# One accumulator tile a bank through the expert stage, with its padding columns written by a product

## The chip, the cores and the metric

The kernel runs on 1 core of a Trainium2 chip. The metric is the device time of one execution in microseconds (us). Engines are named as in the profile: PE is TensorE's matmul, PEld its weight load, DVE VectorE, ACT ScalarE, POOL GpSimd, SP the engine that issues most DMAs.

## What is computed

A decayed linear attention feeds a mixture of experts. The attention's 3072 rows of 512 are routed each to the one expert of eight with the largest logit:

```python
for t in range(S):
    state = gamma[None, :, None, None] * state + np.einsum('bhd,bhe->bhde', k[:, :, t], v[:, :, t])
    y[:, :, t] = scale * np.einsum('bhd,bhde->bhe', q[:, :, t], state)
...
expert_idx = np.argmax(logits, axis=1)
...
for e in range(E):
    mask = expert_idx == e
    h = np.maximum(x[mask] @ w1[e], 0.0)          # w1[e]: 512 x 1024
    out[mask] = gate_w[mask, None] * (h @ w2[e])  # w2[e]: 1024 x 512
```

## The kernel before

The attention runs over 12 blocks of 256 tokens while logits, ranks and a table of slots are made. Then the experts follow one after the other, sorted by their row counts (expert 0 stays first), with room for CAPS = 408, 408, 400, 392, 384, 384, 360, 360 rows. Each engine works through its instructions in the order of the code (`manual_schedule`); only semaphores between engines set the times.

Every float32 product is made of three: weights and activations are split into a high part (`whi`, `xh`, `hh`; cast on ACT) and a low part (`wlo`, `xl`, `hl`; subtraction on DVE), and high x high, high x low and low x high are summed. The weights come in 64 pieces of 512 KB (per expert four of w1, then four of w2), which `load_piece` issues on SP into four buffers `raw`, and which `split` casts on ACT (L217) and subtracts on DVE (L223). A new load into a buffer waits for the L223 that read it.

An expert's first layer makes 8 groups (`ft`) of 12 products (L238) into one accumulator bank each; `hidden` reads it with a relu on ACT (L244, gives `hh`) and then on DVE (L245, gives `hl`). The second layer has two forms. `layer2` makes 4 groups (`dt`) of 24 products (L1021) with the tokens along the columns; `y_turn` (L1027) then transposes the accumulator on DVE in blocks of 32 columns, and so reads up to the next multiple of 32 (288 for 280, 416 for 408). `layer2_rows` (L1063) makes rows directly and needs no transposition. `layer2` is used for experts 0, 1, 2, 3 and 6 (`TURNED`), and for the first 280 rows (`EARLY`) of expert 0.

Accumulators come from `acc_()`: it takes six of the eight PSUM banks in turn (py0, py1, pst0, pst1, b0, b1), and each call makes a new tile in its bank, whose first writer waits until all that used the old tile of the bank are done. The columns between the row count and the next multiple of 32 are cleared by a DVE memset before the products: L1079 for the four `layer2` groups of expert 0 (`early_acc`, 8 columns), L1212 for experts 1, 2, 3 and 6 (four memsets each, of 8, 16, 24 and 24 columns, at `ft` = 6, ahead of `hidden(6)`). As DVE works in order and the memset is the first writer of the tile, the first product of the group waits for all that stands ahead of the memset on DVE.

The order of expert 0's end (L1082 to L1149), in which the work below stands: `layer2` dt 0, then `y_turn` and the remaining `sort_steps` (small DVE operations), dt 1, dt 2; transposes of the late 128 rows (`xr0`, L608 on PE); `split` of piece 8; two groups of the late rows' first layer (L1103, `hr`) with `split` of piece 9 and the gates between them; `turn_hidden(0)` (L1116 on PE, L1118 on ACT, L1119 on DVE); `split` of piece 10; `layer2` dt 3; `turn_hidden(1)`; `split` of piece 11; `x_turn` and `x_low` of expert 1 (L1004, L1005, L1011: they transpose and split the gathered rows `xg`); `layer2_rows` of the late rows; `y_turn(3)`; 16 DMAs of `out_rows` (L1033). Expert 1's rows reach `xg` by gathers (L589, POOL), a write to DRAM (L975) and a reading back (L994), both on SP.

In the loop over experts 1 to 7 (L1177) the next expert's rows are turned and three of its weight pieces split inside the second layer (`next_x`), ahead of `y_turn` on DVE.

Of the kernel before, what the change touches and what calls it, by code (L numbers as in the profile page):

```python
# [13 lines left out]
BF16 = mybir.dt.bfloat16  # L14
# [10 lines left out]
P = 128  # L25
# [11 lines left out]
Q = 32  # L37
# [4 lines left out]
NXC = -(-CAP // Q)  # L42
OV = 352
EARLY = 280
# [61 lines left out]
def retention_moe(ctx: ExitStack, tc: tile.TileContext, q, k, v, emb, tau, w1, w2, const, const16, out):  # L106
    nc = tc.nc

    cp = ctx.enter_context(tc.tile_pool(name="cp", bufs=1))
# [42 lines left out]
    def bank(tag, bufs=1):  # L152
        return ps_.tile([P, 512], F32, name=tag, bufs=bufs)


    turn_of = ["b0", "b1", "b2", "b3"]
    npt, nacc = [-1], [-1]

    def pt_():
        npt[0] += 1  # L160
# [1 line left out]

    def acc_():
        nacc[0] += 1
        return bank(("py0", "py1", "pst0", "pst1", "b0", "b1")[nacc[0] % 6])


    NPC = NE * 8
# [11 lines left out]
    def load_piece(behind=None):  # L180
        g = nload[0]
        if g >= NPC:
            return
        nload[0] += 1
        s, j = divmod(g, 8)
        e = expert[s]
        r = rp.tile([P, 1024], F32, name="raw")
        if s == 0 and j < 4:

            for jj in range(KT):  # L190
                f = P * jj + Q * j
                nc.sync.dma_start(out=r[jj * Q:(jj + 1) * Q], in_=w1[0, f:f + Q, :])
        elif j < 4:
            i = nc.sync.dma_start(out=r, in_=w1r[ds(e * DM + j * P, P), :])
            if behind is not None:
                after(i, behind)
        else:
            i = nc.sync.dma_start(
                out=r.rearrange("p (c d) -> p c d", c=2),
                in_=w2r[ds(e * DF + 2 * (j - 4) * P, 2 * P), :].rearrange("(c p) d -> p c d", p=P))  # L200
            if behind is not None:
                after(i, behind)
        raw_t[g] = r
# [22 lines left out]
    def split():  # L226
        split_cast()()

    def first_layer(e, ft, acc, xh, xl, cols, whole=KT):
        w = cols.stop - cols.start  # L230
        for kt in range(KT):
            wh, wl = piece[e * 8 + kt]
            f = slice(ft * P, (ft + 1) * P)
            terms = ((wh, xh), (wh, xl), (wl, xh))
            if kt >= whole:
                terms = ((wholes[e * 8 + kt], xh.bitcast(F32)), (wh, xl))
            for i, (a, x) in enumerate(terms):
                nc.tensor.matmul(acc[:, :w], a[:, f], x[:, kt, cols], start=(kt + i == 0),  # L238
                                 stop=(kt == KT - 1 and i == len(terms) - 1))
                yield  # L240
# [326 lines left out]
    def run_all(*gs):  # L567
        gs = list(gs)
        while gs:
            gs = [g for g in gs if next(g, gs) is not gs]  # L570
# [14 lines left out]
    def tokens(p, e, c):  # L585
        nc.gpsimd.tensor_copy(out=si[:p, e, c], in_=tb[:p, e, c, 1])
# [299 lines left out]
    hh0 = hp.tile([P, FT, CAP], F32R, name="hh")  # L886
    hl0 = hp.tile([P, FT, CAP], F32R, name="hl")
# [14 lines left out]
    def slots(e):  # L902
        if e not in expert:
            load_expert(e)
        nc.sync.dma_start(out=tb[:, e], in_=tbl[ds(expert[e] * STRIDE, NG * P), :2 + NE].rearrange("(j p) o -> p j o", p=P))
# [65 lines left out]
    def write_rows(e):  # L971
        full, rest = full_rest(e)
        xr, xs = xrs[e], xsd[e % 2]
        for j in range(full if e == 1 else 0):
            nc.sync.dma_start(out=xs[j * P:(j + 1) * P], in_=xr[:, j])  # L975
        if e > 1:
            nc.sync.dma_start(out=xs[:full * P].rearrange("(j p) x -> p j x", p=P), in_=xr[:, :full])
        if rest:
            nc.sync.dma_start(out=xs[full * P:full * P + rest], in_=xr[:rest, full])
# [7 lines left out]
    def gates_of(e):  # L987
        return gates(e, [(P, slice(0, NG), tb[:, e, :, 2:])])
# [25 lines left out]
    def layer2(e, dt, hh, hl, c, acc=None):  # L1014
        acc = acc_() if acc is None else acc
        n = 0
        for kt in range(FT):
            wh, wl = piece[e * 8 + 4 + kt // 2]
            f = slice((2 * dt + kt % 2) * P, (2 * dt + kt % 2 + 1) * P)
            for a, x in ((wh, hh), (wh, hl), (wl, hh)):  # L1020
                nc.tensor.matmul(acc[:, :c], a[:, f], x[:, kt, :c], start=(n == 0), stop=(n == 3 * FT - 1))  # L1021
                n += 1
        return acc

    def y_turn(dt, acc, yt, c):
        nb = -(-c // Q)
        nc.vector.transpose(out=yt[:, :nb, dt], in_=acc[:, :nb * Q].rearrange("p (n b) -> p n b", b=Q))  # L1027
# [46 lines left out]
    gather_rows(1)  # L1074
    tokens(P, 0, slice(3, 4))
    tokens(P, 1, slice(0, NG))
    def early_acc():
        acc = acc_()
        nc.vector.memset(acc[:, EARLY:-(-EARLY // Q) * Q], 0.0)  # L1079
        return acc  # L1080

    for dt in range(3):  # L1082
        acc = layer2(0, dt, hh0, hl0, EARLY, early_acc())
        y_turn(dt, acc, yt0, EARLY)
        if dt == 0:
            run_all(sort_steps)
# [10 lines left out]
    for f in (slice(0, 512), slice(512, 1024)):  # L1097
        acc = acc_()
# [13 lines left out]
    def turn_hidden(f):  # L1112
        ps = pt_()
        o = ps.rearrange("p (k t) -> p k t", k=4)
        for i in range(4):
            nc.tensor.transpose(o[:, i], hr[:, (4 * f + i) * P:(4 * f + i + 1) * P], ident)  # L1116
        kk = slice(4 * f, 4 * f + 4)
        nc.scalar.copy(out=hh0[:, kk, late], in_=o)  # L1118
        nc.vector.tensor_tensor(out=hl0[:, kk, late], in0=o, in1=hh0[:, kk, late].bitcast(F32), op=ALU.subtract)  # L1119

    turn_hidden(0)
    split()
    load_piece()
    acc = layer2(0, 3, hh0, hl0, EARLY, early_acc())
    turn_hidden(1)
    split()
    load_piece()
# [10 lines left out]
    acc = acc2  # L1138
# [38 lines left out]
    for e in range(1, NE):  # L1177
        nxt = e + 1 < NE
        c = CAPS[e]
        cols = slice(0, c)  # L1180
        hh = hp.tile([P, FT, CAP], F32R, name="hh")
        hl = hp.tile([P, FT, CAP], F32R, name="hl")
        gsteps = iter(())
        last = None
        for ft in range(FT):
            acc = last or acc_()
            for _ in first_layer(e, ft, acc, *xTs[e], cols):
                pass
            if ft == 0 and e + 2 < NE:
                slots(e + 2)  # L1190
            if nxt and ft == 1:
                write_rows(e + 1)
            if not nxt and ft == 2:
                nc.gpsimd.drain()
            if ft in (0, 1, 3, 5, 6):
                split()
                load_piece()
            if pend and not pend[5] and ft < 4:
                out_rows(pend[1], pend[2], ft, pend[3])
            if nxt and ft == 3:  # L1200
                read_quarters(e + 1)
            if ft == 1:
                gsteps = gates_of(e)
                next(gsteps)
            if ft > 2:
                for _ in range(3):
                    next(gsteps, None)
            if ft == FT - 2 and TURNED[e]:
                last, *accs = [acc_() for _ in range(KT + 1)]
                if c % Q:  # L1210
                    for a in accs:
                        nc.vector.memset(a[:, c:-(-c // Q) * Q], 0.0)  # L1212
            hidden(ft, acc, hh, hl, cols)
        done, pend = pend, None

        def finish_two():
            if done:
                for j, n in done[4][:2]:
                    finish(done[0], j, n, done[2])
                del done[4][:2]  # L1220

        og = mp.tile([P, NG, DM], F32, name="og", bufs=2)
        if TURNED[e]:
            yt = mp.tile([P, NXC, KT, Q], F32, name="yt", bufs=2)
            for dt in range(KT):
                acc = layer2(e, dt, hh, hl, c, accs[dt])
                if dt < 2:
                    finish_two()
                if dt < 2:
                    squares(e + 1, dt)  # L1230
                if dt < 3:
                    next_x(e + 1, dt)
                if dt == 1:
                    next_rows(e + 2)
                y_turn(dt, acc, yt, c)
            pend = (e, yt, og, c, groups_of(e), False)
        else:
            for j, n in groups_of(e):
                acc = layer2_rows(e, j, n, hh, hl, slice(j * P, j * P + n))
                finish_two()  # L1240
                if nxt:
                    if j < 2:
                        squares(e + 1, j)
                    next_x(e + 1, j)
                    if j == 1:
                        next_rows(e + 2)
                finish(e, j, n, og, acc[:n])
# [90 lines left out]
```

## Time and profile before

| | us |
|---|---|
| median of 3 runs | 421.93 (420.23 to 426.4) |
| the profiled execution | 419.81 |
| its span in the trace | 418.0 |
| around the span (419.81 - 418.0) | 1.8 |
| PE busy | 393.6 (94%) |
| DVE busy | 255.2 (61%) |
| ACT busy | 211.5 (51%) |

An engine's busy time is the time in which it had an instruction under way. PE's is no measure of its speed: the granted clock of a stretch stands beside it (1.00 is 2.4 GHz, 0.50 is 1.2 GHz). A wait is put down to the releaser that came last.

### The profile page before, as it was taken

Reading aid. Unit: us, or ns where it says so; the run is one execution under the profiler, and the core shown is the slowest. Engines: PE = TensorE matmul, PEld = TensorE weight load, DVE = VectorE, ACT = ScalarE, POOL = GpSimd, SP = SyncE. Lnnn points to the kernel's source line nnn. Section 1 sums busy time; section 2 is a strip of 40 time slices with the busy share of each in tenths; the row PEclk is TensorE's granted clock in tenths of the full one; section 3 lists DMA queues with packets and bytes.
Section 4 is the critical chain, followed back from the end, with each engine's and each line's share of the span. In section 5 each row is a group of like instructions: output and inputs, shape, how many; then the busy total and the mean of one; then the engine's idle time right before and its main releaser. Section 6 shows DMA issues by size and latency. Waiting matters only on the chain.

```text
span 418.0 us, 9549 instructions
## 1 busy us (share of the span) xinstructions
PE 393.6 (94%) x3648; PEld 360.0 (86%) x3648; DVE 255.2 (61%) x546; ACT 211.5 (51%) x378; POOL 157.3 (38%) x176
## 2 busy tenths in 40 slices
PE   7999999999987796997999999999999999999993
PEld 3998889888876676897999999999889989999971
DVE  4497877879788243762676296186376474775400
ACT  3565567557746033644544565375475465643410
POOL 2567485788562310151260260161147053000130
PEclk9999999999999898999999999999999999999997
DMA  7898998986677963269596977969778958941121
GB/s 224 252 295 258 255 266 247 253 229 162 165 209 187 344 142 99 71 169 321 183 285 196 245 266 231 247 230 300 170 256 306 284 176 299 258 148 46 36 96 50
DMA packets 88195, 88.39 MB, mean 211 GB/s; under 512 B 10525, under 2 KB 66717, under 8 KB 88140
## 3 DMA queue, kind: packets, MB, share of 16 engines
q1 hardware_dynamic: 83100, 74.60, 62.5%
q0 software_dynamic: 4864, 13.03, 9.1%
q8 instruction: 30, 0.49, 0.5%
q14 instruction: 25, 0.20, 0.2%
q10 hardware_dynamic: 176, 0.07, 0.1%
HBM read 64.99 MB, written 18.79 MB: 200 GB/s over the span
## 4 chain that ended last, share of the span: by engine, by line
PE 50%; issue 5%; SPq 5%; DVE 3%; ACT 2%; DMA 1%; POOL 1%; POOLq 0%; DVEq 0%; ACTq 0%
PE pst L1021 10%; PE b L238 8%; PE py L238 7%; PE pst L238 5%; PE py L1021 5%; PE b L1021 5%; SPq L1033 5%; PE pst L1063 4%; PE py L1063 4%; POOL out_dram L1045 1%; DMA raw<-in_moe_w_dram 1%; ACT whi L217 1%; DVE wlo L223 1%; PE py L1103 1%; DMA og<-yt 0%
## 5 line engine op out<-in xcount | busy, mean ns | idle before, releaser
L223 DVE TENSOR_TENSOR wlo<-raw,whi 128x1024 fp32r<-128x1024 f32 x64 | 77.9, 1219 | 22.3 <-ACT whi L217 21.2
L1045 POOL DMA_INDIRECT out_dram<-og,si x28 | 28.7, 1024 | 122.2 <-ACT og L1038 63.9
L217 ACT CAST whi<-raw 128x1024 fp32r<-128x1024 f32 x64 | 66.3, 1043 | 4.9 <-DMA raw<-in_moe_w_dram 4.8
L589 POOL DMA_INDIRECT xr<-xd,gi x25 | 33.1, 1324 | 30.7 <-issue 27.8
L1021 PE MATMUL pst<-hh,whi 128*128 128x280 f32 (+4 forms) x80 | 27.9, 349 | 9.8 <-DVE pst L1079 9.8
L1004 DVE STREAM_TRANSPOSE xt<-xg 128x384 f32<-128x384 f32 (+1 forms) x28 | 15.7, 579 | 33.6 <-DMA xg<-xs 33.5
L338 POOL TENSOR_TENSOR hl<-wlo,cst 128x512 f32<-128x512 f32 x22 | 22.7, 1050 | 30.7 <-DMA wlo<-in_k_dram 19.8
L395 DVE TENSOR_TENSOR pm<-b,mask 128x512 f32<-128x512 f32 x48 | 29.7, 681 | 6.2 <-PE b L375 6.2
L238 PE MATMUL b<-xl,whi 128*128 128x384 f32 (+5 forms) x96 | 32.3, 336 | 0.0
L238 PE MATMUL b<-xh,wlo 128*128 128x384 f32 (+5 forms) x96 | 32.0, 333 | 0.0
L238 PE MATMUL b<-xh,whi 128*128 128x384 f32 (+5 forms) x96 | 32.0, 333 | 0.0
L238 PE MATMUL py<-xl,whi 128*128 128x384 f32 (+5 forms) x88 | 30.0, 341 | 0.0
L560 POOL DMA_INDIRECT tbl<-zt,sloti x24 | 24.9, 1037 | 10.1 <-issue 5.3
L238 PE MATMUL py<-xh,whi 128*128 128x384 f32 (+5 forms) x84 | 28.0, 333 | 0.0
L257 POOL TENSOR_TENSOR r<-r,half 128x4 f32<-128x4 f32 (+1 forms) x9 | 9.0, 996 | 50.3 <-DVE r L256 50.1
L238 PE MATMUL py<-xh,wlo 128*128 128x384 f32 (+5 forms) x84 | 27.9, 332 | 0.0
L1005 ACT CAST xh<-xt 128x384 fp32r<-128x384 f32 (+4 forms) x28 | 14.2, 510 | 26.9 <-DVE xt L1004 26.6
L1021 PE MATMUL pst<-hl,whi 128*128 128x280 f32 (+4 forms) x80 | 27.5, 344 | 0.0
L1021 PE MATMUL pst<-hh,wlo 128*128 128x280 f32 (+4 forms) x80 | 27.4, 343 | 0.0
L375 PE MATMUL b<-qT,kT 64*128 64x128 f32 x384 | 26.3, 280 | 1.1 <-DVE kT L349 0.9
L375 PEld LDWEIGHTS b<-qT,kT 64*128 64x128 f32 x384 | 23.5, 188 | 2.9 <-ACT kT L349 1.1
L1021 PEld LDWEIGHTS pst<-hh,whi 128*128 128x128 f32 x80 | 16.4, 205 | 10.4 <-issue 7.9
(225 smaller groups left out, 1045.6 us busy)
## 6 DMA issues: line engine op xcount, KB each, us to landing
raw<-in_moe_w_dram SPq DMA_DIRECT2D x60, 512.0 KB
whi<-in_q_dram SPq DMA_DIRECT2D x24, 256.0 KB
xd<-x SPq DMA_DIRECT2D x48, 128.0 KB
wlo<-in_k_dram SPq DMA_DIRECT2D x11, 512.0 KB
xs<-xr SPq DMA_DIRECT2D x6, 768.0 KB
whi<-in_v_dram SPq DMA_DIRECT2D x6, 512.0 KB
wlo<-in_v_dram SPq DMA_DIRECT2D x6, 512.0 KB
xg<-xs SPq DMA_DIRECT2D x16, 192.0 KB
```

The lines of the kernel that those rows point to most:

```text
L217: nc.scalar.copy(out=views[1], in_=views[0])
L223: nc.vector.tensor_tensor(out=views[2], in0=views[0], in1=views[1].bitcast(F32), op=ALU.subtract)
L238: nc.tensor.matmul(acc[:, :w], a[:, f], x[:, kt, cols], start=(kt + i == 0), stop=(kt == KT - 1 and i == len(terms) - 1))
L338: return eng.tensor_tensor(out=ks_r[:, m % 3, s, h], in0=kin[m % 3][:, h, s], in1=w[:, h], op=ALU.mult)
L375: nc.tensor.matmul(psc[a][:, j], kTs[m][a * D:(a + 1) * D, j, u].rearrange("p s c -> p (s c)"), q_cols(m, a, j, u), start=True, stop=True, ...
L395: o.append(nc.vector.tensor_tensor(out=pm, in0=psc[a], in1=w, op=ALU.mult))
L560: i = nc.gpsimd.indirect_dma_start(out=tbl[:, :], out_offset=bass.IndirectOffsetOnAxis(ap=sloti[:, n:n + 1], axis=0), in_=zt[:, n], in_off ...
L589: return nc.gpsimd.indirect_dma_start(out=xr[:n, j, :], out_offset=None, in_=xd[:rows_, :], in_offset=bass.IndirectOffsetOnAxis(ap=gi[:n, ...
L1021: nc.tensor.matmul(acc[:, :c], a[:, f], x[:, kt, :c], start=(n == 0), stop=(n == 3 * FT - 1))
L1033: nc.sync.dma_start(out=og[h * Q:(h + 1) * Q, :n, i * P:(i + 1) * P], in_=yt[i * Q:(i + 1) * Q, h:nb:NQ].rearrange("p n t a -> p n (t a)"))
L1045: i = nc.gpsimd.indirect_dma_start(out=out[:, :], out_offset=bass.IndirectOffsetOnAxis(ap=si[:n, e, j:j + 1], axis=0), in_=og[:n, j, :], i ...
L1063: nc.tensor.matmul(acc[:s, :], x[:, kt, at], a, start=(n == 0), stop=(n == 3 * FT - 1))
```

## The change

`acc_()` keeps one tile for each of its six banks. The first time that it takes a bank it makes the tile, and PE writes zeros into the columns 280 to 415 with one bf16 product of a zeroed tile `blank` (128 x 136, cleared once by POOL near the start of the program). Afterwards the same tile is handed out again, and the clearings L1079 and L1212 on DVE are gone. Columns past an expert's row count then hold zeros or what an earlier, wider group left there; those columns belong to rows that are not stored. Nothing else moves in the order of any engine.

```diff
-    npt, nacc = [-1], [-1]
+    npt, nacc, accs_ = [-1], [-1], {}
+    blank = cp.tile([P, NXC * Q - EARLY], BF16, name="blank")
+    nc.gpsimd.memset(blank, 0.0)
...
     def acc_():
         nacc[0] += 1
-        return bank(("py0", "py1", "pst0", "pst1", "b0", "b1")[nacc[0] % 6])
+        tag = ("py0", "py1", "pst0", "pst1", "b0", "b1")[nacc[0] % 6]
+        if tag not in accs_:
+            a = accs_[tag] = bank(tag)
+            nc.tensor.matmul(a[:, EARLY:NXC * Q], blank[:, :P], blank, start=True, stop=True)
+        return accs_[tag]
...
-    def early_acc():
-        acc = acc_()
-        nc.vector.memset(acc[:, EARLY:-(-EARLY // Q) * Q], 0.0)
-        return acc
-
     for dt in range(3):
-        acc = layer2(0, dt, hh0, hl0, EARLY, early_acc())
+        acc = layer2(0, dt, hh0, hl0, EARLY)
...
-    acc = layer2(0, 3, hh0, hl0, EARLY, early_acc())
+    acc = layer2(0, 3, hh0, hl0, EARLY)
...
                 last, *accs = [acc_() for _ in range(KT + 1)]
-                if c % Q:
-                    for a in accs:
-                        nc.vector.memset(a[:, c:-(-c // Q) * Q], 0.0)
```

## Rows read from the trace of the kernel before

**Rows 1.** The head of the profile's page.

```profile
span 418.0 us, 9549 instructions
```

**Rows 2.** The table of waits of PE over the whole span: who waited for whom; us in total, times, the longest.

```profile
PE pst L1021 <- DVE pst L1079: 9.8, 3, 4.6
PE py L1021 <- DVE b L1212: 2.6, 1, 2.6
...
PE b L1021 <- DVE b L1079: 0.6, 1, 0.6
```

**Rows 3.** Busy time of each engine by stretch (from:to in us, length; PE, PEld, DVE, ACT and POOL busy with their instructions; then the granted clock, the DMA share and GB/s).

```profile
...
131.60:134.60 3.00, 0.04 (x1) 0.01 (x1) 2.87 (x6) 0.72 (x3) 1.73 (x2) 1.00 0.34 36
...
134.60:138.00 3.40, 3.34 (x24) 3.14 (x24) 0.00 (x0) 0.00 (x0) 2.44 (x5) 1.00 0.96 340
...
140.20:143.40 3.20, 3.20 (x14) 3.20 (x15) 0.00 (x0) 0.00 (x0) 0.46 (x3) 0.50 0.95 361
...
189.60:192.30 2.70, 0.06 (x2) 0.05 (x1) 1.54 (x7) 2.63 (x5) 0.00 (x0) 1.00 1.05 411
...
192.30:378.40 186.10, 186.10 (x1010) 179.64 (x1011) 111.23 (x211) 98.73 (x173) 54.82 (x52) 1.00 0.79 238
...
```

**Rows 4.** The timeline of PE and DVE at the end of expert 0, from 131 to 166 us: start, duration, engine, line, operation; in brackets the idle time before it and what ended it.

```profile
131.35 0.29 PE L238 MATMUL py<-xh,wlo 128*128 128x280 f32 x1
...
132.49 1.20 DVE L223 TENSOR_TENSOR wlo<-raw,whi 128x1024 fp32r<-128x1024 f32 x1
...
133.62 0.79 DVE L245 SCALAR_TENSOR_TENSOR hl<-py,hh 128x280 fp32r<-128x280 f32 x2
134.41 0.07 DVE L1079 MEMSET pst<- 128x8 f32 x1
...
134.83 0.30 PE L1021 MATMUL pst<-hl,whi 128*128 128x280 f32 x1
...
134.96 0.30 PE L1021 MATMUL pst<-hh,wlo 128*128 128x280 f32 x1
...
140.07 0.07 DVE L1079 MEMSET pst<- 128x8 f32 x1
...
148.89 0.49 PE L608 MATMUL b<-ident,xr 128*128 128x128 f32 x3
...
155.29 0.60 PE L1116 MATMUL b<-ident,hr 128*128 128x128 f32 x4
...
159.00 1.23 DVE L223 TENSOR_TENSOR wlo<-raw,whi 128x1024 fp32r<-128x1024 f32 x1 [0.25 <-ACT whi L217]
160.23 0.07 DVE L1079 MEMSET pst<- 128x8 f32 x1
...
160.44 0.43 PE L1021 MATMUL pst<-hh,whi 128*128 128x280 f32 x1 [4.55 <-DVE pst L1079]
...
165.14 0.60 PE L1116 MATMUL b<-ident,hr 128*128 128x128 f32 x4
165.49 0.48 PE L1063 MATMUL b<-whi,hh 128*128 128x512 f32 x1
```

**Rows 5.** The timeline of ACT and DVE where expert 1 goes from its first to its second layer.

```profile
189.67 1.04 ACT L217 CAST whi<-raw 128x1024 fp32r<-128x1024 f32 x1 [2.54 <-DMA raw<-in_moe_w_dram]
...
190.75 1.23 DVE L223 TENSOR_TENSOR wlo<-raw,whi 128x1024 fp32r<-128x1024 f32 x1 [1.87 <-ACT whi L217]
...
192.07 0.07 DVE L1212 MEMSET py<- 128x8 f32 x1
...
192.56 0.57 DVE L245 SCALAR_TENSOR_TENSOR hl<-py,hh 128x408 fp32r<-128x408 f32 x1
```

**Rows 6.** The timeline of SP's DMA issues from 133 to 169 us: start, time from the first to the last issue of the run, line, what is loaded.

```profile
133.21 2.57 SPq L194 DMA_DIRECT2D raw<-in_moe_w_dram  x4
...
147.08 1.89 SPq L994 DMA_DIRECT2D xg<-xs  x4
152.20 16.76 SPq L198 DMA_DIRECT2D raw<-in_moe_w_dram  x4
...
```

**Rows 7.** The view of DMA issues, from 133.0 to 133.9 us: POOL's gather of the late rows (L589), count, us from issue to landing.

```profile
xr<-xd,gi POOLq DMA_INDIRECT x1, 6.4
```

**Rows 8.** Busy time by stretch again (columns as in rows 3), where expert 1's rows are read back.

```profile
148.50:152.50 4.00, 3.97 (x22) 3.11 (x20) 2.60 (x7) 2.33 (x7) 0.16 (x1) 1.00 1.03 203
152.50:154.00 1.50, 1.50 (x8) 1.22 (x7) 0.00 (x0) 1.30 (x2) 1.12 (x2) 1.00 0.28 92
```

**Rows 9.** The timeline of DVE and PE at the start of experts 1 to 3: the first turning of the next expert's rows, then the last split and the product that needs it.

```profile
168.48 1.10 DVE L1004 STREAM_TRANSPOSE xt<-xg 128x416 f32<-128x416 f32 x2
...
201.46 1.10 DVE L1004 STREAM_TRANSPOSE xt<-xg 128x416 f32<-128x416 f32 x2 [8.33 <-DMA xg<-xs]
...
236.77 1.10 DVE L1004 STREAM_TRANSPOSE xt<-xg 128x416 f32<-128x416 f32 x2 [7.77 <-DMA xg<-xs]
...
245.45 1.21 DVE L223 TENSOR_TENSOR wlo<-raw,whi 128x1024 fp32r<-128x1024 f32 x1
...
247.20 0.34 PE L238 MATMUL b<-xh,wlo 128*128 128x392 f32 x1
```

**Rows 10.** Groups of instructions by line and shape, of PE and of POOL: count, busy us, mean ns of one, idle time before them.

```profile
L719 PE MATMUL b<-x 128*128 128x512 bf16 x10 | 4.5, 632 | 1.3 <-DVE x L700 1.3
...
L727 POOL MEMSET enT<- 128x128 f32 x1 | 0.2, 198 | 0.0
```

## The prediction

> **What bounds the kernel now.** I read the head of the page first: the span is 418.0 us [rows 1], and the profiled execution took 1.8 us more. Then the table of PE's waits: nearly all that PE waits for after the attention is one kind of instruction, the memsets of accumulator padding on DVE, with 9.8 us and 0.6 us for L1079 and 2.6 us for L1212 [rows 2]. A memset of 8 columns lasts 0.07 us; what costs is what stands ahead of it on DVE. The stretches show the rest: from 192.3 to 378.4 us PE has no gap at all, at full clock, so the memsets of experts 2, 3 and 6 hold nobody up; and from 140.2 to 143.4 us PE counts as busy throughout, but at a granted clock of 0.50, behind two gaps [rows 3]. So the named waits (13.0 us) are less than what hangs on them. Everything behind the gaps is late by their sum, as PE is the bound from there on; I follow each gap to what would end it next.
>
> **Gap 1, before dt 0.** PE issues its last L238 at 131.35 us and can go on at about 131.6, but dt 0 waits for the memset of 134.41, behind two low splits and three L245 [rows 4]. Without the memset the 24 products go in the order of kt. The first 18 need only pieces and halves that DVE has done when it starts on piece 7 at 132.49, so they run from 131.7 at 0.13 us each (134.83 to 134.96) and end at 134.0. The last six need piece 7's low part (132.49 + 1.20 = 133.69) and the last two L245, done at 134.41 [rows 4]. With the 0.14 us from the memset's end to PE's start (160.30 to 160.44), the last two products start at 134.55 and 134.68, and dt 1 may start at 134.81.
>
> **Gaps 2 and 3, before dt 1 and dt 2.** The memset at 140.07 stands behind `y_turn` and the sort steps, and dt 2's behind the next `y_turn`. Neither group needs them for its products: the hidden rows are complete and the banks were read out long before. Both follow without a gap, 24 x 0.128 = 3.07 us each, to 137.88 and 140.95. The first transposition of the late rows starts at 148.89 now [rows 4]. The gain so far is 148.89 - 140.95 = 7.94 us, with the slow clock's part in it: as PE no longer stands still, I let it keep the full clock.
>
> What is late next there? The gathered late rows: issued before 133.9, 6.4 us to landing [rows 7], so there by 140.3, 0.65 us ahead. Piece 8, cast on ACT right behind, was issued first of four at 133.21 [rows 6], and by 138.0 DMA had moved 3.4 us x 340 GB/s = 1156 KB [rows 3] against 512 KB for the piece and 256 KB for the gather. Both hold, the first barely.
>
> **Gap 4, before dt 3.** `turn_hidden(0)` starts on PE at 155.29 and takes 0.35 us (165.14 to 165.49, the same four transpositions later), so dt 3 could begin at 155.64; it waits until 160.44 for the memset at 160.23, behind piece 10's low split [rows 4], which dt 3 doesn't read. That is 4.80 us. Then dt 3 starts at the slow clock: 165.14 - 160.44 = 4.70 us against 3.07, another 1.63. Together 6.43 us, and 7.94 + 6.43 = 14.37 us. The 8 us of ACT and DVE work that stood idle behind dt 3 (the second half of the hidden rows, piece 11, `x_turn`) moves with PE.
>
> **What is late next at expert 1.** `x_turn` of expert 1 starts at 168.48 [rows 9] and would be wanted at 168.48 - 14.37 = 154.1. Its rows are read back by four DMAs from 147.08 [rows 6], and this doesn't move: it hangs on gathers, not on PE. The DMA engines are full (1.03) from 148.5 to 152.5 and quiet (0.28) after it [rows 8], so the rows are there at 152.5 and 1.6 us are left. But pieces 12 and 13, issued from 152.20 now because they wait for piece 8's split, would come at about 149.0, right behind the reads on SP. If they share the engines with them, 1 MB more at 361 GB/s [rows 3] is 2.9 us, and the reads end at up to 155.4: 1.3 us too late. If not, nothing. I take 0.5 us of loss, between both ends.
>
> The Trainium skill (DMA: Bandwidth & Descriptors, Queues, rings and completion order) says that all of SP's DMAs go through one row of rings, and that each engine takes descriptors in ring order. By that rule the later pieces cannot get ahead of the reads, and the loss would be near 0 rather than 0.5. No row here shows such a pair.
>
> **Gap 5, expert 1's second layer.** The four L1212 memsets at 192.07 stand behind the low split of 190.75, which waits for a piece cast at 189.67, when its load had just landed [rows 5]. That piece is expert 2's first; expert 1's second layer doesn't read it. Without the memsets PE goes on at once, at about 189.7; by columns a product takes 0.13 x 408 / 280 = 0.19 us (an estimate from rows 4), so the 23rd, the first to ask for the last L245 (192.56 + 0.57 = 193.13), comes at 189.7 + 22 x 0.19 = 193.9. So the whole 2.6 us are won here. But they are not kept: expert 2's rows land at 201.46, with DVE waiting, and all that follows them on DVE hangs on SP and DMA, not on PE. How near PE is to this chain is seen one expert later, where it is nearest: the last split ends at 245.45 + 1.21 = 246.66 and PE asks for it at 247.20 [rows 9]. PE can run ahead by 0.54 us and no more; I keep 0.5 of the 2.6.
>
> **What is added.** Six products of 136 bf16 columns, all before 131.35 us, as the first layer of expert 0 takes each bank once. No row has that shape: from above, the warm-up product of 512 columns, 4.5 us / 10 = 0.45 us [rows 10], 2.7 us in all; from below nothing, where PE waits anyway. By columns it is 0.13 x 136 / 280 = 0.06 us, 0.4 us in all. In gap 1 there is no cover for it: the 22 products from 131.7 end at 134.51, just when the last L245 lets the 23rd go (134.55). I take 0.4. The memset on POOL (nearest row 0.20 us for 128x128 [rows 10]) is done in the first microseconds, more than 100 us before a product reads it, and its cover is the wait for the first loads. The removed memsets free DVE for 20 x 0.07 = 1.4 us, nearly all off the path: nothing.
>
> **The sum.** 7.94 + 6.43 - 0.5 + 0.5 - 0.4 = 14.0 us. From the profiled execution, 419.81 - 14.0 = 405.8; from the median of the runs, which is 2.1 us higher, 421.93 - 14.0 = 407.9. I predict between them, 406.8.
>
> **Rivals.**
> 1. The chain of the next expert's rows gives way (its DMAs find freer engines), and all of gap 5 stays: 14.37 + 2.6 - 0.4 = 16.6 us, 403.2 to 405.3, say 404.3. Against it: DVE waits 8 us for it at 201.46 and at 236.77 [rows 9]. Chance 0.12.
> 2. Data for expert 1 comes late. The rows are wanted at 154.1, and each microsecond after that is lost; if expert 1 could not start earlier than about 165 us, only gaps 1 to 3 would pay, 7.94 - 0.4 = 7.5 us, 412.3 to 414.4, say 413.4. For it: the DMA engines are full; against it: the reads are over by 152.5 now. Chance 0.12, of which 0.10 end within 2% (8.4 us).
> 3. Slower: a tile that is kept instead of made anew could be tracked more coarsely, so that each group's first product waits for DVE's reading of the group before it, in another bank. The price would be at least a group's L245, 0.57 us [rows 5], at each of some 90 groups, 51 us, less 14 won: about 445 us. It decides from 0.25 us a group (90 x 0.25 = 22.5, the 14.0 won and 8.4 more). Against it: PE's table names no wait of L238 for DVE or ACT, though all its banks come round in six groups, and a bank's last reader is the same whether the tile is new or kept. Chance 0.04.
> 4. The forecast, 0.72.
>
> So faster by over 2% (what a measurement here can tell from no change) 0.12 + 0.72 + 0.02 = 0.86, within 2% 0.10, slower 0.04. The range: 402.5 holds rival 1 and leaves out a little; upward, the late rows (1.3), the products (2.7) and a small part of rival 2 give 411.5. It leaves out about 2 in 10.
>
> **What would show it.** Right: no memset among PE's waits; dt 0 to dt 2 without a gap at full clock, the transposition of the late rows at about 141; dt 3 at about 147.7; expert 1's first L238 at about 157.2; its second layer without a gap; a new gap of PE of about 2 us in the first group of expert 2 or 3, ended by a DVE low split or L1011. Wrong: a wait of PE for `xg`, `raw` or the gather between 140 and 157, a clock under 1.00 there, or PE waiting for DVE at group after group.

## The result and the profile after

The changed kernel takes 404.48 us (median, 402.9 to 406.18), the kernel before 421.08 on the same chip: a ratio of 0.9615 [0.9543, 0.9686], faster. The forecast was 406.8 in a range of 402.5 to 411.5. The profiled execution took 403.01 us against 419.81, so 16.8 us less; the sum of the forecast was 14.0. Line numbers of the changed kernel are 6 higher up to about L1080 (L238 is L244, L1021 is L1027, L1004 is L1010).

The head of the page after, with the share of PE and the granted clock in 40 slices:

```profile
span 401.3 us, 9543 instructions
...
PE 389.6 (97%) x3654; PEld 356.6 (89%) x3654; DVE 255.2 (64%) x526; ACT 211.9 (53%) x378; POOL 153.6 (38%) x177
...
PEclk9999999999999999999999999999999999999998
```

The table of waits of PE after (who waited for whom; us in total, times, longest):

```profile
PE b L725 <- DVE x L706: 1.3, 1, 1.3
...
PE b L244 <- DVE wlo L229: 0.5, 1, 0.5
```

The memsets that stood first in this table, 13.0 us in all [rows 2], are gone, and what is left after the attention is one wait of 0.5 us for a low split. The stretches after, at the times at which [rows 3] showed gaps and the slow clock (columns as there):

```profile
131.60:134.60 3.00, 3.00 (x26) 3.00 (x25) 2.32 (x5) 0.67 (x3) 1.60 (x3) 1.00 0.53 82
134.60:138.00 3.40, 3.40 (x28) 3.40 (x28) 1.87 (x10) 0.00 (x0) 2.59 (x3) 1.00 0.98 344
140.20:143.40 3.20, 3.17 (x19) 2.53 (x18) 1.77 (x6) 2.23 (x7) 0.00 (x0) 1.00 0.89 351
175.00:178.00 3.00, 3.00 (x18) 3.00 (x17) 1.65 (x3) 2.74 (x5) 0.00 (x0) 1.00 1.04 391
```

PE is busy in each, at a granted clock of 1.00. The first stretch had 0.04 us of PE work before, the third a clock of 0.50 [rows 3]; the fourth is where expert 1 now goes to its second layer.

The timeline of PE after, at the steps of the forecast (start, duration, line, operation, idle time before it):

```profile
131.44 0.30 PE L244 MATMUL py<-xh,wlo 128*128 128x280 f32 x1
131.58 0.29 PE L1027 MATMUL pst<-hh,whi 128*128 128x280 f32 x1
...
134.68 0.29 PE L1027 MATMUL pst<-hh,whi 128*128 128x280 f32 x1
...
137.77 0.29 PE L1027 MATMUL b<-hh,whi 128*128 128x280 f32 x1
...
140.86 0.49 PE L614 MATMUL b<-ident,xr 128*128 128x128 f32 x3
...
147.61 0.38 PE L1027 MATMUL pst<-hh,whi 128*128 128x280 f32 x1
...
156.80 0.35 PE L244 MATMUL b<-xh,whi 128*128 128x408 f32 x1
...
175.15 0.35 PE L1027 MATMUL py<-hh,whi 128*128 128x408 f32 x1
...
194.81 0.34 PE L244 MATMUL b<-xl,whi 128*128 128x400 f32 x1
195.62 0.45 PE L244 MATMUL b<-xh,wlo 128*128 128x400 f32 x1 [0.47 <-DVE wlo L229]
195.91 0.34 PE L244 MATMUL py<-xh,whi 128*128 128x400 f32 x1
```

From 131.44 to 140.86 there is no gap: dt 0, dt 1 and dt 2 take 3.1 us each. The late rows follow at 140.86 (148.89 before [rows 4]), dt 3 at 147.61 (160.44 [rows 4]), expert 1 at 156.80, its second layer at 175.15. The table cuts every profiled execution at five such starts (us; the kernels below `after` are the experiments of the next section): *a* from the last first-layer product of expert 0 (131.35 before) to the first transposition of the late rows, *b* from there to expert 1's first product, *c* to its second layer, *d* to the second group of expert 2, *e* to the end of the span. What lies ahead of *a* is the attention.

| kernel | a | b | c | d | e |
|---|---|---|---|---|---|
| before | 17.54 | 22.27 | 21.12 | 20.10 | 205.62 |
| after | 9.42 | 15.94 | 18.35 | 20.76 | 205.39 |
| after_again | 9.43 | 15.96 | 19.69 | 20.79 | 205.40 |
| after_five | 9.70 | 15.96 | 18.43 | 21.50 | 205.65 |
| kept_tiles_memsets | 20.15 | 22.79 | 20.89 | 21.54 | 205.26 |
| fresh_tiles_products | 9.96 | 16.04 | 20.14 | 20.02 | 206.19 |
| memsets_ahead | 10.77 | 15.95 | 18.34 | 20.85 | 205.33 |
| dt012_memsets_back | 18.28 | 15.94 | 18.35 | 21.26 | 205.41 |
| dt3_memset_back | 9.42 | 22.80 | 18.32 | 21.00 | 205.61 |
| loop_memsets_back | 9.43 | 15.94 | 21.16 | 21.64 | 205.28 |
| loop_memsets_five | 9.42 | 15.95 | 22.24 | 21.65 | 205.74 |
| blank_products_x17 | 9.42 | 15.94 | 18.33 | 22.92 | 206.19 |

So the gain of the profiled execution over the kernel before is 17.54 - 9.42 = 8.12 us in *a* (gaps 1 to 3 with their slow clock), 6.33 in *b* (gap 4), 2.77 in *c* (gap 5), -0.66 in *d*, 0.23 in *e*, less the 0.09 us by which the last first-layer product came later: 16.7, the difference of the spans.

### The profile page after: what moved, and what is told of

It reads as the page before. It is cut to its first block, busy times and chain, and to the rows that moved or that the text cites. A ratio compares the mean times of both kernels' runs of the same rounds, so it can differ in the third digit from the quotient of the medians.

```text
span 401.3 us, 9543 instructions
## 1 busy us (share of the span) xinstructions
PE 389.6 (97%) x3654; PEld 356.6 (89%) x3654; DVE 255.2 (64%) x526; ACT 211.9 (53%) x378; POOL 153.6 (38%) x177
## 4 chain that ended last, share of the span: by engine, by line
PE 60%; DVE 10%; DMA 10%; issue 7%; SPq 6%; POOL 3%; ACT 3%; POOLq 0%; DVEq 0%; ACTq 0%
PE b L244 8%; PE py L244 8%; PE pst L244 7%; PE py L444 6%; PE pst L1027 5%; PE pst L1069 4%; PE py L1069 4%; PE py L1027 4%; PE b L381 4%; PE b L1027 3%; DMA xg<-xs 3%; SPq L1039 2%; PE pst L415 2%; DMA xr<-xd,gi 2%; PE b L350 2%
## 5 line engine op out<-in xcount | busy, mean ns | idle before, releaser
L595 POOL DMA_INDIRECT xr<-xd,gi x25 | 30.8, 1233 | 24.5 <-ACT sq L278 16.3
L1010 DVE STREAM_TRANSPOSE xt<-xg 128x384 f32<-128x384 f32 (+1 forms) x28 | 15.7, 579 | 30.4 <-DMA xg<-xs 30.2
L244 PE MATMUL b<-xh,wlo 128*128 128x384 f32 (+5 forms) x96 | 32.1, 334 | 0.5 <-DVE wlo L229 0.5
L244 PE MATMUL b<-xl,whi 128*128 128x384 f32 (+5 forms) x96 | 32.2, 336 | 0.0
L244 PE MATMUL b<-xh,whi 128*128 128x384 f32 (+5 forms) x96 | 32.1, 335 | 0.0
L244 PE MATMUL py<-xl,whi 128*128 128x384 f32 (+5 forms) x88 | 29.9, 340 | 0.0
L244 PE MATMUL py<-xh,whi 128*128 128x384 f32 (+5 forms) x84 | 28.0, 333 | 0.0
L244 PE MATMUL py<-xh,wlo 128*128 128x384 f32 (+5 forms) x84 | 27.8, 331 | 0.0
L1027 PE MATMUL pst<-hh,whi 128*128 128x280 f32 (+4 forms) x80 | 26.2, 328 | 0.0
L1027 PE MATMUL pst<-hl,whi 128*128 128x280 f32 (+4 forms) x80 | 26.1, 326 | 0.0
L1027 PE MATMUL pst<-hh,wlo 128*128 128x280 f32 (+4 forms) x80 | 26.1, 326 | 0.0
L444 PE MATMUL py<-pm,vs 128*64 128x128 f32 x384 | 24.7, 277 | 0.4 <-DVE vs L394 0.4
```

The costliest lines, as they stand in the source:

```text
L444: nc.tensor.matmul(pys[m][u][o * D:(o + 1) * D, j], lhsT, rhs, start=first, stop=True, skip_group_check=True)
L595: return nc.gpsimd.indirect_dma_start(out=xr[:n, j, :], out_offset=None, in_=xd[:rows_, :], in_offset=bass.IndirectOffsetOnAxis(ap=gi[:n, ...
```

## The experiments

The theory: the time hung on where the clearings stood in DVE's order. Its rivals: it hung on a tile being made anew for each group, or on a DVE write into the bank at all. A second question came from the result: how much of gap 5 is kept.

### Tiles kept, all memsets left (kept_tiles_memsets)

```diff
-    npt, nacc = [-1], [-1]
+    npt, nacc, accs_ = [-1], [-1], {}
...
-        return bank(("py0", "py1", "pst0", "pst1", "b0", "b1")[nacc[0] % 6])
+        tag = ("py0", "py1", "pst0", "pst1", "b0", "b1")[nacc[0] % 6]
+        if tag not in accs_:
+            accs_[tag] = bank(tag)
+        return accs_[tag]
```

This is the kernel before with this alone; L1079 and L1212 are L1082 and L1215 here.

> The kernel before with one change: the six accumulator tiles are kept and handed out again; all 20 memsets stay where they are, and there are no padding products. Theory (the gain is the removal of DVE memsets that stand behind unrelated DVE work): as before, 419 to 423 us, with PE's waits for L1079 and L1212 at about 10.4 and 2.6 us again. Rival A (keeping a tile, instead of releasing and making it, is what frees PE): 403 to 407 us. Rival B (kept tiles are tracked more coarsely and cost): above 424 us.

Measured: 422.9 us, ratio 0.9989 [0.9943, 1.0035]. PE's waits are those of [rows 2]:

```profile
PE pst L1024 <- DVE pst L1082: 9.7, 3, 4.5
PE py L1024 <- DVE b L1215: 2.4, 1, 2.4
```

Keeping the tiles does nothing by itself, for good or ill: the waits are the same. Column *a* is 2.6 us longer than before (20.15 against 17.54) at these same waits, because the granted clock over it was lower, 0.75 against 0.90 (the last section has more on this). With that the slower rival of the forecast (a kept tile tracked more coarsely, about 445 us) has no ground either: no new wait, group after group, is there.

### New tiles, a product in each of the 20 groups (fresh_tiles_products)

```diff
+    blank = cp.tile([P, NXC * Q - EARLY], BF16, name="blank")
+    nc.gpsimd.memset(blank, 0.0)
...
+    def pad_product(a):
+        nc.tensor.matmul(a[:, EARLY:NXC * Q], blank[:, :P], blank, start=True, stop=True)
...
-        nc.vector.memset(acc[:, EARLY:-(-EARLY // Q) * Q], 0.0)
+        pad_product(acc)
...
-                        nc.vector.memset(a[:, c:-(-c // Q) * Q], 0.0)
+                        pad_product(a)
```

> The kernel before with one change: each of the 20 memsets is replaced by a padding product on PE (136 bf16 columns) into the same fresh tile; tiles are still made anew at each call. Theory: as the changed kernel, less its six products, plus 20 of about 0.07 us: 403 to 407 us. Rival A (kept tiles): no gain, 419 to 423 us.

Measured: 407.85 us, 0.85 above the expected range, ratio 0.9664 [0.9626, 0.9701]. One wait is new:

```profile
PE b L170 <- DVE hl L250: 1.3, 1, 1.3
```

Nearly all of the gain is there without one tile kept. The 1.3 us are what clearing a new tile can cost even on PE: the product of the second layer's last bank is issued at `ft` = 6, and that bank still holds hidden group 5, which DVE has not read. It happened once, at expert 1. Column *c* shows it, 20.14 us against 18.35, of which 0.7 us comes back in *d*. So in the trace writing the padding once has a small worth of its own; the times of the two kernels do not tell them apart.

### All memsets kept, but earlier in DVE's order (memsets_ahead)

```diff
+    ahead = [cleared(t) for t in ("pst0", "pst1", "b0")]
     split()
...
-        acc = layer2(0, dt, hh0, hl0, EARLY, early_acc())
+        nacc[0] += 1
+        acc = layer2(0, dt, hh0, hl0, EARLY, ahead[dt])
         y_turn(dt, acc, yt0, EARLY)
+        if dt == 1:
+            ahead.append(cleared("pst1"))
...
-    acc = layer2(0, 3, hh0, hl0, EARLY, early_acc())
+    nacc[0] += 1
+    acc = layer2(0, 3, hh0, hl0, EARLY, ahead[3])
...
+            if ft == FT - 2 and TURNED[e]:
+                last, *accs = [acc_() for _ in range(KT + 1)]
+                if c % Q:
+                    for a in accs:
+                        nc.vector.memset(a[:, c:-(-c // Q) * Q], 0.0)
             if ft in (0, 1, 3, 5, 6):
                 split()
```

`cleared` makes a tile in the named bank and clears its 8 columns; the block of the loop is moved up, from behind the split to ahead of it.

> The kernel before with all 20 memsets and fresh tiles, but each memset moved ahead in DVE's order: those of dt 0 to 2 before the split of piece 7, that of dt 3 behind the y_turn of dt 1, and L1212 before the split at ft = 6. Theory (what counts is what stands ahead of the memset on DVE, not the memset): as the changed kernel, 402 to 406 us, no wait of PE for a memset over 0.3 us. Rival C (the freed DVE time or the number of writers pays): 415 to 422 us.

Measured: 405.3 us, ratio 0.9625 [0.9568, 0.9682]. Twenty DVE memsets, each in a new tile, and the whole gain. PE's waits:

```profile
PE pst L1027 <- DVE b L898: 1.1, 1, 1.1
...
PE b L238 <- DVE wlo L223: 0.6, 1, 0.6
```

One wait of 1.1 us for a memset is left ahead of dt 0 (*a* is 10.77, 1.35 over the changed kernel's), which I had not expected over 0.3. But the position of the memsets is what counted, not that DVE clears.

### The parts put back one by one (dt3_memset_back, dt012_memsets_back)

Both are the changed kernel, with the memset again ahead of dt 3 alone, or of dt 0, dt 1 and dt 2 alone (`early_acc` is that of the kernel before, but on the kept tiles):

```diff
-    acc = layer2(0, 3, hh0, hl0, EARLY)
+    acc = layer2(0, 3, hh0, hl0, EARLY, early_acc())
```

```diff
-        acc = layer2(0, dt, hh0, hl0, EARLY)
+        acc = layer2(0, dt, hh0, hl0, EARLY, early_acc())
```

> The changed kernel with one of its memsets put back, that of dt 3 of expert 0 (8 columns, 0.07 us). Theory: gap 4 comes back whole, 4.8 us of standing still and 1.6 us of slow clock behind it, 6.3 us in all, less up to 0.6 us that expert 2's first group no longer waits: 408.7 to 409.5 us where the changed kernel takes 403.0. Rival (the clock stays at full speed, as only this one gap is left): 4.8 us, 407.8. Rival (data for expert 1 would set its start anyway): under 2 us.

> The changed kernel with the memsets of dt 0, 1 and 2 of expert 0 put back. Theory: gaps 1 to 3 come back, 8.0 us to the first transposition of the late rows, with the granted clock at 0.50 for about 3 us behind gap 2; about 411 us where the changed kernel takes 403.0. With the other run, 6.3 + 8.0 = 14.3 us should be the whole of what expert 1's start gained. Rival (gaps overlap, one gives back what the other takes): the two losses together clearly under 14 us.

Measured: 411.55 us and 412.52 us, against 405.86 for the changed kernel beside them (after_again): 5.7 and 6.7 us by the medians, each good to some 3 us, as the four runs of a kernel spread by 2 to 4 us. The columns say more: *b* is 22.80 against 15.96 with dt 3's memset back, 6.84 us (the forecast's gap 4: 6.43), and *a* 18.28 against 9.43 with the other three, 8.85 us (gaps 1 to 3: 7.94). No other column moves by more than 0.5 us, except *c* of after_again (below); but these two profiles are also 2.5 and 2.6 us longer ahead of *a*, in the attention, which the edits do not touch. By the columns the two losses add up to 15.7 us, so the gaps do not overlap; the medians alone (12.4) would not have told. The wait of dt 3 in dt3_memset_back, by its timeline:

```profile
153.95 0.60 PE L1027 MATMUL pst<-hh,whi 128*128 128x280 f32 x1 [4.47 <-DVE pst L1085]
```

and the stretch behind it:

```profile
153.95:158.15 4.20, 4.20 (x18) 4.20 (x19) 0.00 (x0) 0.00 (x0) 0.00 (x0) 0.50 1.05 349
```

A wait of 4.47 us, then 4.2 us at a granted clock of 0.50, the lower level: about half of these 4.2 us is lost as well. By column *b* a single 8-column memset costs 6.8 us.

### The loop's memsets put back (loop_memsets_back, after_five, loop_memsets_five)

```diff
                 last, *accs = [acc_() for _ in range(KT + 1)]
+                if c % Q:
+                    for a in accs:
+                        nc.vector.memset(a[:, c:-(-c // Q) * Q], 0.0)
```

> The changed kernel with the 16 memsets of the loop (L1212) put back at their old place; those of expert 0 stay out. Theory as the trace of the changed kernel shows it: PE waits about 2.7 us at expert 1's second layer again, of which 0.5 to 0.7 us is won back at expert 2's first group, so 2.0 us slower than the changed kernel (403.0 in its profile): 405 us in the profiled execution. Theory of the prediction (PE can run ahead of the next expert's rows by 0.5 us only): 0.5 us slower, 403.5 us. If expert 2's rows are first turned 15.7 us earlier than in the kernel before here too, their coming earlier does not hang on PE's being ahead in expert 1's second layer; at 14.4 us earlier it does.

Measured: 406.21 us, ratio 0.964 [0.9586, 0.9694]; the changed kernel itself (0.9615) lies within that interval, so this time settles nothing. Nor does the sign that was looked for in its trace: expert 2's rows are turned at 185.89 us, 15.57 earlier than before, which was to mean that they don't hang on PE; but this profile was 1.28 us ahead of the first one already at expert 1's first product. Counted from there the turning comes after 30.37 us, 30.30 in the kernel before, 28.96 after the change, 30.33 in after_again and 28.80 in kept_tiles_memsets, which goes with neither answer. The pair was taken again, with more rounds and the changed kernel on the same chip:

> The changed kernel again, next to the same with L1212's memsets, so that the two are timed on one chip. Theory 1 (my forecast: the chain of the next expert's rows lets PE keep only 0.5 us of expert 1's gap): this kernel is 0.5 us faster than its neighbour. Theory 2 (the chain is not fixed, and the gap stays won with the slow clock behind it): 2.5 to 3.5 us faster. In the profile both give no wait of PE for a memset; theory 1 a wait of about 2 us at the start of expert 2, theory 2 one under 1 us.

> The changed kernel with the 16 memsets of L1212 put back. Both theories: a wait of PE of 2.4 to 2.8 us for a memset ahead of expert 1's second layer, and none for a memset anywhere else. Theory 1: 0.5 us slower than its neighbour, because PE waits less at expert 2 in return. Theory 2: 2.5 to 3.5 us slower, with PE at a granted clock under 1.00 for a stretch behind the wait.

Measured: 413.04 us (410.96 to 414.69) without them, ratio 0.9619 [0.9573, 0.9664]; 415.24 us (414.23 to 417.33) with them, ratio 0.9679 [0.9638, 0.972]. The medians differ by 2.2 us; the means of the six runs each, 412.85 and 415.40, by 2.55, with a 95% interval of 0.8 to 4.3 worked out from their spread. That leaves out theory 1's 0.5 us, if by little, and holds theory 2's 2.5 to 3.5. In the traces *c* + *d* is 43.89 us with the memsets and 39.93 without (loop_memsets_back 42.80, after 39.11); in loop_memsets_five some 1.1 us of the difference is another wait, for expert 1's rows (161.68 us, DVE stood 1.09 us for them), so about 3 to 3.7 us hang on the memsets. At expert 2's first group PE waits for the low split in after_five, for less than the 1 us of theory 2, where theory 1 had about 2 us:

```profile
204.57 0.45 PE L244 MATMUL b<-xh,wlo 128*128 128x400 f32 x1 [0.69 <-DVE wlo L229]
```

The wait for the memsets in loop_memsets_five:

```profile
185.41 0.42 PE L1027 MATMUL py<-hh,whi 128*128 128x408 f32 x1 [2.57 <-DVE b L1213]
```

and the stretches behind it:

```profile
183.00:186.00 3.00, 0.58 (x3) 0.62 (x4) 2.11 (x8) 3.00 (x6) 0.43 (x1) 1.00 1.01 397
186.00:190.00 4.00, 4.00 (x16) 3.90 (x15) 0.26 (x1) 1.22 (x4) 1.59 (x2) 0.58 1.03 257
```

Behind the same wait the kernel before had 1.00 [rows 3]; here it is 0.58 for 4 us, 1.7 us lost on top. kept_tiles_memsets, with a wait of 2.4 us there, has it too:

```profile
194.50:198.50 4.00, 4.00 (x14) 3.91 (x15) 0.85 (x2) 1.79 (x5) 2.02 (x2) 0.59 1.12 270
```

### Seventeen times the products (blank_products_x17)

```diff
-            nc.tensor.matmul(a[:, EARLY:NXC * Q], blank[:, :P], blank, start=True, stop=True)
+            for _ in range(17):
+                nc.tensor.matmul(a[:, EARLY:NXC * Q], blank[:, :P], blank, start=True, stop=True)
```

> The changed kernel with each of its six padding products made 17 times over (102 instead of 6). Theory of the sum: 0.06 us each without cover, 96 x 0.06 = 5.8 us, less what falls into PE's waits for DVE at the end of the attention (the first 17 wait anyway, about 1 us): 4 to 6 us slower than the changed kernel. Rival (they are hidden where PE waits): under 1.5 us. Rival (a product that starts a bank costs its full 0.23 us): over 15 us.

Measured: 410.81 us, 4.95 over after_again, so 4.95 / 96 = 0.05 us for each added product, but with an uncertainty of over 3 us on the 4.95; and the profiled execution is 9.9 us longer than that of after_again, of which 8.5 lie ahead of *a*, where the products are, and 2.1 in *d*, where none is. The timeline gives the price more closely. A row of 17 and the product behind it:

```profile
125.50 1.18 PE L171 MATMUL pst<-blank 128*128 128x136 bf16 x17
126.49 0.37 PE L245 MATMUL pst<-xh,whi 128*128 128x280 f32 x1
```

17 of them hold the stream for 126.49 - 125.50 = 0.99 us, 0.058 each. (The first row, 117.85 to 119.71 us, met a granted clock of 0.50 and held it for 1.86 us; the other five took 0.97 to 0.99.) At 0.058 the six of the changed kernel cost 0.35 us. Its groups of them, by the view that groups instructions (count, busy us, mean ns):

```profile
L170 PE MATMUL py<-blank 128*128 128x136 bf16 x2 | 0.5, 233 | 0.0
L170 PE MATMUL b<-blank 128*128 128x136 bf16 x2 | 0.5, 232 | 0.0
L170 PE MATMUL pst<-blank 128*128 128x136 bf16 x2 | 0.5, 226 | 0.0
```

The mean of 0.23 us is one product from start to end; as they are pipelined, only the 0.04 to 0.06 us to the next one's start count.

### The changed kernel once more (after_again)

> The changed kernel as it is, for comparison on the same chip: 402 to 407 us by every theory.

Measured: 405.86 us, ratio 0.9595 [0.9512, 0.9679]. Its column *c* is 1.3 us longer than the first profile's. DVE's timeline tells why:

```profile
154.61 1.10 DVE L1010 STREAM_TRANSPOSE xt<-xg 128x416 f32<-128x416 f32 x2 [1.27 <-DMA xg<-xs]
```

Here DVE waits 1.27 us for expert 1's rows, whose read-back SP issued at 147.90; in the first profile SP issued it at 146.75, and DVE found the rows there. SP in after_again:

```profile
147.90 1.88 SPq L1000 DMA_DIRECT2D xg<-xs  x4
```

SP and DVE in the first profile:

```profile
146.75 1.88 SPq L1000 DMA_DIRECT2D xg<-xs  x4
...
154.15 1.10 DVE L1010 STREAM_TRANSPOSE xt<-xg 128x416 f32<-128x416 f32 x2
...
185.76 1.10 DVE L1010 STREAM_TRANSPOSE xt<-xg 128x416 f32<-128x416 f32 x2 [7.14 <-DMA xg<-xs]
...
194.35 1.22 DVE L229 TENSOR_TENSOR wlo<-raw,whi 128x1024 fp32r<-128x1024 f32 x1
```

(The last two lines, of expert 2, are used in the next section.) In after_again PE then waits three times for the low halves of the turned rows. Its table counts 0.7 us, less than column *c* lost, because it counts from the modelled end of the product before: by their starts (155.92 and 156.51, for one) these products come 0.6 us behind the one before instead of 0.18. So this wait is at the edge: it comes and goes from one execution to the next.

## Why the prediction was right, and where it was off

- **Gaps 1 to 3** (7.94 us): 8.03 by the late rows' transposition, 8.12 in *a*. The forecast let the last two products of dt 0 wait for DVE until 134.55; DVE was 0.49 us earlier here (its last L251 below ends at 133.92, before at 134.41 [rows 4]) and they did not. Putting the three memsets back cost 8.85. The gathered late rows, forecast to be there 0.65 us ahead, held nobody up.

```profile
133.13 0.79 DVE L251 SCALAR_TENSOR_TENSOR hl<-py,hh 128x280 fp32r<-128x280 f32 x2
```

- **Gap 4** (4.80 and 1.63 us of slow clock, 6.43): 6.33 in *b*, and 6.84 when its memset alone was put back. That this wait is charged twice, once as idle time and once at the lower clock, was right, and the second part was a quarter of the term.
- **Late rows of expert 1** (0.5 lost, between 0 and 1.3): nothing in the first profile and in after_five, 1.3 us in after_again, 1.1 in loop_memsets_five. The losses fell between the bounds, but that the upper one came out as 1.3 was luck: it was worked out from weight pieces that share the DMA engines with the reads, and they do not slow them. The traces record each packet of a DMA. The read-back is 1664 packets of 512 bytes. In the three traces in which no packet of the next piece started before the reads were over (before, kept_tiles_memsets, dt012_memsets_back) the last of them ended 5.3 to 5.7 us after SP's first issue; in the nine with pieces issued right behind, 5.3 to 5.8 us. In the first profile after the change the pieces were issued from 148.84 us, and their first packet started at 151.65, when the reads were all but done (152.17). This agrees with the rule of the Trainium skill (DMA: Bandwidth & Descriptors, Queues, rings and completion order) that each engine takes the descriptors of SP's ring in their order.

  What the forecast left out is what follows the last packet. Where DVE waited, it started 1.0 us behind it (153.60 to 154.61 in after_again) and 0.9 (160.74 to 161.68 in loop_memsets_five), about 6.7 us after the issue. So the rows were not there at 152.5 in the kernel before, but by this at about 153.7 (152.69 + 1.0, an estimate), 0.4 us ahead of the 154.1 at which they would be wanted, and not 1.6. What decides is when SP can issue the read-back: DVE was free to turn the rows 7.4 us after it in the first profile (146.75 to 154.15), 6.7 in after_five, 5.4 in after_again (147.90 to 153.34). That issue waits for the gathers and for the writes behind them, and not for PE.
- **Gap 5**, the step that was mis-sized: "PE can run ahead by 0.54 us and no more; I keep 0.5 of the 2.6". In the first profile PE won 2.77 us there and kept 2.11. The two numbers behind the 0.5 were both wrong. First, the room: I took it from expert 3, where it is least, but what PE wins at expert 1 meets the chain at expert 2. In the timeline of the kernel before, of DVE and of PE:

```profile
210.05 1.22 DVE L223 TENSOR_TENSOR wlo<-raw,whi 128x1024 fp32r<-128x1024 f32 x1
...
212.20 0.34 PE L238 MATMUL b<-xh,wlo 128*128 128x400 f32 x1
```

  the last split ends at 211.27 and PE asks for it at 212.20: 0.93 us of room. Second, the chain: I took it to move with PE's start of expert 1 (14.36 us), and its `x_turn` moved by 201.46 - 185.76 = 15.70 us, as the read-back took 8.01 us from SP's issue to the turning instead of 9.24. Then 17.13 - 15.70 - 0.93 = 0.50 us is what PE has to wait at expert 2, and the timeline after shows 0.47 (0.63 by the starts, 194.81 and 195.62 where 0.18 is usual, about what *d* lost). The forecast named the place and the releaser of this new wait rightly, and its size (2 us) wrongly. At expert 3 PE does not wait. How much is kept is not one number, though: *c* + *d* is 41.22 us before and 39.11 after, but 39.93 in after_five and 40.48 in after_again, where the late rows are in it (1.3); and in the two kernels with the old wait it is 42.43 (kept_tiles_memsets) and 42.80 (loop_memsets_back), as the slow clock follows the wait there.
- **Added products** (0.4 us): 0.04 to 0.06 each, 0.24 to 0.35 in all. The estimate by columns (0.06) was right and the upper bound of 2.7 far off.
- **The sum**: 14.0 against 16.8 in the first profile; of the 2.8, 1.6 is gap 5 (2.11 for 0.5), 0.5 the late rows, 0.3 what lies ahead of *a* (0.09 lost where 0.4 was forecast for the products), 0.2 column *e*; gaps 1 to 4 are within 0.2 each. What came is nearest to the first rival, worked out as 16.6 us, 404.3, and given 0.12; that the forecast holds all the same is due to the range, which had been drawn to hold that rival. Against it I had put DVE's waits of 8 us for the chain. They are real and still there (7.14 us at 185.76), but they show that DVE has nothing else to do, not that PE is near the chain.
- **Open**: why the read-back of expert 2's rows takes 7.9 to 9.4 us in most traces (11.0 in loop_memsets_five). It was 9.24, 9.35 and 10.96 in three of the four profiles in which PE stood at gap 5, 7.92 in the fourth, and 7.97 to 8.75 in the eight without; one exception in four is too much to call the gap its cause. By the packets the difference is a tail: of the 1664, those that started later than 7.0 us after the issue are 6 after the change, 24 before it and 64 in loop_memsets_five, where the last ended after 9.9 us. What holds them up was not tried.

## What to carry to other kernels

Here the first writer of a tile brought all that stood ahead of it on its engine with it: a 0.07 us memset on DVE cost 6.8 us because a split of data that the group does not read stood ahead of it. To find such waits, look in PE's table for releasers that do almost no work; then write the padding on the engine that consumes the bank, once, or move the clearing ahead of the long work. And to size how much of a removed wait is kept, follow it to the next point where the late engine asks for something, and take the room there, not the smallest room found anywhere.

## What the hardware showed that was not expected

A wait of 2.4 to 2.7 us of PE at the same place was followed by a granted clock of 1.00 in one trace (before) and of 0.58 to 0.67 over 4 us in three; so such a wait costs what it lasts, or some 1.3 to 1.7 us more, and one profile does not show which. The first gap shows the same: after 2.98 us before dt 0 the kernel before went on at 1.00 [rows 3], and after 2.99 us kept_tiles_memsets went on at 0.50:

```profile
133.95 0.57 PE L1024 MATMUL pst<-hh,whi 128*128 128x280 f32 x1 [2.99 <-DVE pst L1082]
...
134.00:137.40 3.40, 3.40 (x15) 3.40 (x16) 0.00 (x0) 0.00 (x0) 2.44 (x5) 0.50 0.91 324
```

With the same three waits (the first of them 2.4 to 3.0 us) column *a* was 17.54 us (before), 18.28 (dt012_memsets_back) and 20.15 (kept_tiles_memsets), at a mean granted clock of 0.90, 0.81 and 0.75. So the 8.12 us in *a* hold against the one profile of the kernel before; against the other two it would be 8.9 and 10.7.

And one chip needed about 8 us more for the attention (after_five has the last first-layer product at 139.26 us, after at 131.44), with each of *a* to *e* within 0.8 us of the first profile's: the ratio to the kernel before is the same there (0.9619), but times of different chips do not compare.
